# An FFT and mixer block on one core: the second channel product of most chunks from seven half-size products instead of eight

## The chip, the cores and the metric

The kernel runs on one core of one Trainium2 chip. The metric is the device time of one execution in microseconds; the time before is a median of three runs. The engines are named as in the profile: PE is TensorE's matmuls and PEld its weight loads, DVE is VectorE, ACT is ScalarE, POOL is GpSimd, SP is SyncE, which here only issues DMAs.

## The reference

```python
def _attn_ref(x):                       # x: (8, 3008, 256)
    X = np.fft.fft(x, axis=1)
    X = np.fft.fft(X, axis=2)
    return X.real.astype(np.float32)

def _moe_ref(x, w_tok1, w_tok2, w_ch1, w_ch2):
    xt = x.transpose(0, 2, 1)
    h = np.maximum(xt @ w_tok1, 0.0) @ w_tok2      # (3008,256), (256,3008)
    u = x + h.transpose(0, 2, 1)
    h2 = np.maximum(u @ w_ch1, 0.0) @ w_ch2        # (256,1536), (1536,256)
    return (u + h2).astype(np.float32)

reference = _moe_ref(_attn_ref(x), ...)
```

The change concerns the last product, `relu(u @ w_ch1) @ w_ch2`, and the sum with `u` behind it.

## The kernel before, in words

The eight batches run one behind the other. Each has a front part (the Fourier transforms as small matrix products `pz`, `pw`, `py`, the token mixing `pt` and `pu`), which ends in `ut`: u, transposed, with the 256 channels in two halves of 128 partitions and the tokens along the free axis. The channel part takes `ut` in 6 chunks of 512 tokens (448 in the sixth).

A chunk has 12 slots, one for each block `ct` of 128 of the 1536 hidden channels. In each slot `mm1` makes one block of the first channel product: two matmuls of 512 columns into the PSUM tile `pc` (three buffers), and a relu that moves it to the fp16 tile `c1`, on VectorE for every third block (line 565) and on ScalarE for the others (line 563). `c1` has two buffers: while the slots of a chunk make its `c1`, the second channel product `mm2` takes the `c1` of the chunk before (`prev`). At slots 2, 5, 8 and 11 it makes 128 tokens each: 12 matmuls with `c1` as weights and 256 columns of `wc2` moving (line 590), into half of a PSUM tile `po`. Behind each second of them VectorE adds `uT`, which is u with tokens on partitions, and writes `osb` (lines 598 and 599, drawn as L90, the helper's line); at slot 11 SP stores `osb` (line 612). `uT` comes from DMA transposes that SP issues at slot 4 of the chunk's own slots (line 574).

The instructions are issued in the order in which the Python loops write them, each engine runs its own in that order, and semaphores connect them. The front part of the next batch is a generator; between the slots `take` draws from it evenly, 45 pieces over the 71 slots of a batch (in batch 0 over the last 40), so that each slot carries 0.6 of a piece. The columns of a batch's transforms are added in pairs first (`fold`: adds of 96x512 fp16 within SBUF), for batches 0 and 1 on VectorE, for the later ones on GpSimd, all in one piece when 8 front pieces are through (slot 13), followed by the loads of x for the batch after (`load_x`). At the end of a batch's chunks GpSimd moves 64 leftover columns of `c1` between an even batch and the odd one behind it (`tail1`).

Of the kernel before, what the change touches and what calls it, by code (L numbers as in the profile page):

```python
# [36 lines left out]
def kernel(  # L37
# [34 lines left out]
    def dram(t, offset, ap):  # L72
        return bass.AP(tensor=t, offset=offset, ap=ap)
# [31 lines left out]
    def gdma(out_, in_):  # L105
        G.dma_start(out=out_, in_=in_)  # L106
# [193 lines left out]
    wc2 = const.tile([P, NCT, D], FP16, tag="wc2")  # L300

    HC = DCH // 2

# [7 lines left out]
    def load_rest():  # L311
        load_wc1(0)
        for th in range(2):
            gdma(w2n[:, th, :], dram(w2_t, th * P * S, [[S, P], [1, S]]))
        load_wc1(1)
        gdma(wc2[:], dram(wc2_t, 0, [[D, P], [P * D, NCT], [1, D]]))

    yrow = const.tile([3, 2, 8, 64], FP16, tag="yrow")
    state = {}
# [25 lines left out]
    NFOLD = 17  # L345

    def filler(n):
        pw = ps_out("filler")
        for _ in range(n):
            nc.tensor.matmul(pw[:, 0:P], lhsT=ident[:], rhs=lrot[:], start=True,  # L350
                             stop=True)
# [197 lines left out]
            for c in (2, 1, 0, 3, 4, 5):  # L549
                yield from tok2(c)  # L550

    def mm1(b, c, c1, ct, cts=None):
        ut = state[b]["ut"]
        n = min(CW, S - CW * c)
        cts = cts or (ct,)
        pcs = [ps_mm("pc") for _ in cts]
        for h in range(2):
            for pc, ct in zip(pcs, cts):
                nc.tensor.matmul(pc[:, 0:n], lhsT=wc1[:, h, ct * P:(ct + 1) * P],  # L559
                                 rhs=ut[:, c, h, 0:n], start=(h == 0), stop=(h == 1))  # L560
# [8 lines left out]
    def turn_u(b, c):  # L569
# [4 lines left out]
            nc.sync.dma_start_transpose(out=uT[:, 0:n // P, h, :], in_=ut[:, c, h, 0:n])  # L574
        return uT

    def mm2(b, c, c1, uT, ks, box):
        last = c == 5
        if last and b % 2 == 0 and ks == 3:
            return  # L580
        if ks == 0:
            box["osb"] = work.tile([P, 4, D], FP32, tag="osb", name="osb", bufs=3)
        osb = box["osb"]
        fine = last and b == BB - 1
        if ks % 2 == 0 or fine:
            box["po"] = ps_out("po")
        po = box["po"]
        o = 0 if fine else D * (ks % 2)
        for ct in range(NCT):
            nc.tensor.matmul(po[:, o:o + D], lhsT=c1[:, ct, ks * P:ks * P + P],  # L590
                             rhs=wc2[:, ct, :], start=(ct == 0), stop=(ct == NCT - 1))
        end = ks % 2 == 1 or last and b % 2 == 0 and ks == 2 or fine
        if end:
            k0, n = (ks, 1) if fine else (ks & ~1, 1 + ks % 2)
            src = po[:].rearrange("p (k d) -> p k d", k=2)[:, 0:n]
            uf = uT[:].rearrange("p k h d -> p k (h d)")[:, k0:k0 + n]
            dst = osb[:, k0:k0 + n]
            tt(dst[:, :, 0:129], src[:, :, 0:129], uf[:, :, 0:129], AT.add)
            tt(dst[:, :, 129:256], src[:, :, 129:256], uf[:, :, 255:128:-1], AT.add)
        if fine:  # L600
            for i in range(2 if ks < 3 else 1):
                (nc.sync if i == 0 else nc.scalar).dma_start(
                    out=dram(out_t, (b * S + 8 * c + i + 2 * ks) * D, [[NQ * D, 64], [1, D]]),
                    in_=osb[64 * i:64 * i + 64, ks, :])
            if ks == 3:
                nc.scalar.dma_start(
                    out=dram(out_t, ((b - 1) * S + NQ - 1) * D, [[NQ * D, 64], [1, D]]),
                    in_=osb[64:128, 3, :])
        elif ks == 3 or last and b % 2 == 0 and ks == 2:
            for i in range(2):  # L610
                nk = 4 if not last or b % 2 and i == 0 else 3
                nc.sync.dma_start(
                    out=dram(out_t, (b * S + 8 * c + i) * D,
                             [[NQ * D, 64], [2 * D, nk], [1, D]]),
                    in_=osb[64 * i:64 * i + 64, 0:nk, :])
            if last and b % 2:
                nc.sync.dma_start(
                    out=dram(out_t, ((b - 1) * S + NQ - 1) * D, [[NQ * D, 64], [1, D]]),
                    in_=osb[64:128, 3, :])

    def take(g, n):
        for _ in range(n):
            next(g, None)
# [26 lines left out]
    for k in range(6):  # L650
# [9 lines left out]
    w2v[1] = w2r[:]  # L660

    NFRONT = 45
    own_at = {1: 1, 2: 1, 4: 1, 12: 1, 15: 1, 18: 1, 20: 1, 22: 1, 24: 1, 27: 1, 30: 1, 33: 1,
              36: 1, 39: 1}
    prev = None
    for b in range(BB):
        nxt = front(b + 1) if b + 1 < BB else iter(())
        fold1 = fold(1, V) if b == 0 and BB > 1 else iter(())
        first, done, folded = (31 if b == 0 else 0), 0, False
        for c in range(NCH):  # L670
            c1 = work.tile([P, NCT, CW], FP16, tag="c1", name="c1", bufs=2)
            uT = None
            box = {}
            for ct in range(NCT):
                slot = NCT * c + ct
                if b == 0 and slot < 3:
                    if slot == 0:
                        mm1(b, c, c1, ct, range(3))
                else:
                    mm1(b, c, c1, ct)  # L680
                if ct == 4:
                    uT = turn_u(b, c)
                if prev is not None and ct % 3 == 2:
                    mm2(*prev, ct // 3, pbox)
                if b == 0:
                    take(own, own_at.get(slot, 0))
                    if 10 <= slot < 27:
                        take(fold1, 1)
                    if slot == 27 and BB > 2:
                        load_x(2)  # L690
                    if slot in (31, 33, 35, 37):
                        th, hb = (slot - 31) // 4, (slot - 31) // 2 % 2
# [16 lines left out]
            prev, pbox = (b, c, c1, uT), box  # L709
    for s in range(4):  # L710
        mm2(*prev, s, pbox)

# [29 lines left out]
```

## Time and profile before

| | |
|---|---|
| median of 3 runs | 627.99 us (627.88 to 628.25) |
| profiled execution | 628.33 us, span 626.6 us, clock 0.997 |
| PE busy | 608.9 us, 97% |
| PEld busy | 420.9 us, 67% |
| DVE busy | 344.8 us, 55% |
| ACT busy | 293.2 us, 47% |
| POOL busy | 170.4 us, 27% |

Rows of the profile give, for a group of instructions, the line, the engine, output<-inputs, the shape, the count, the busy time in us and the mean ns of one, then the idle time of the engine just before them and what ended it. A line can be a helper's: all adds of two tensors have L90, whatever engine they are on. Timeline rows begin with the start and the length in us. PE rows of matmuls overlap with one another, so the pitch of a matmul is read from the starts.

### The profile page before, as it was taken

How to read it: one execution, taken by the hardware profiler on the slowest of the kernel's cores; microseconds unless marked ns; L12 is line 12 of the kernel's file. 1: busy time of each engine (PE TensorE's matmuls, PEld its weight loads, DVE VectorE, ACT ScalarE, POOL GpSimd, SP SyncE). 2: the span in 40 equal slices, each digit the busy share in tenths (PEclk: the TensorE clock that was granted, in tenths of full speed). 3: DMA queues.
4: the chain of work that ended last, by engine and by line, in shares of the span. 5: the costliest groups of instructions: out<-in, count | busy, mean ns of one | idle time of the engine just before them, and what ended most of it. 6: DMA issues, size and time to landing. Idle time of an engine off the chain costs nothing.

```text
span 626.6 us, 11701 instructions
## 1 busy us (share of the span) xinstructions
PE 608.9 (97%) x4753; PEld 420.9 (67%) x4753; DVE 344.8 (55%) x728; ACT 293.2 (47%) x573; POOL 170.4 (27%) x231
## 2 busy tenths in 40 slices
PE   4899999999999999999999999999999999999997
PEld 3556676677667776667666776666766677666666
DVE  8668647634764356544665446653466535653343
ACT  8643553464435543454534544356443554344441
POOL 8401890292012900166010850039000000000000
PEclk9899999999999999999999999999999999999999
DMA  8993855338324482336432294252223334342434
GB/s 156 210 171 64 147 79 124 70 69 160 53 52 92 76 139 54 85 54 133 108 68 51 57 170 81 48 92 53 51 52 66 87 51 52 80 67 57 89 65 105
DMA packets 83366, 55.46 MB, mean 89 GB/s; under 512 B 53746, under 2 KB 80050, under 8 KB 82546
## 3 DMA queue, kind: packets, MB, share of 16 engines
q1 hardware_dynamic: 76816, 36.82, 30.8%
q0 software_dynamic: 6176, 17.63, 15.4%
q8 instruction: 37, 0.61, 0.4%
q10 hardware_dynamic: 320, 0.26, 0.2%
q14 instruction: 17, 0.14, 0.1%
HBM read 35.26 MB, written 24.64 MB: 96 GB/s over the span
## 4 chain that ended last, share of the span: by engine, by line
PE 95%; DMA 2%; DVE 1%; POOL 1%; ACT 0%; issue 0%; DVEq 0%
PE po L590 39%; PE pc L559 39%; PE pu L495 7%; PE pt L517 3%; PE pw L448 2%; DMA w1m<-in_moe_w_tok_dram 2%; PE py L474 2%; PE pz L424 1%; PE pw L450 1%; PE ph L405 0%; PE ph L403 0%; POOL xm L109 0%; DVE ix L86 0%; POOL w1p L106 0%; POOL w1m L106 0%
## 5 line engine op out<-in xcount | busy, mean ns | idle before, releaser
L559 PE MATMUL pc<-ut,wc 128*128 128x512 f16 (+1 forms) x1152 | 307.0, 375 | 0.8 <-ACT c L97 0.5
L97 ACT ACTIVATE c<-pc 128x512 f16<-128x512 f32 (+1 forms) x384 | 215.0, 587 | 195.2 <-PE pc L559 174.8
L590 PE MATMUL po<-wc,c 128*128 128x256 f16 x2256 | 276.3, 273 | 0.0
L590 PEld LDWEIGHTS <-c 128*128 128x128 f16 x2256 | 220.6, 98 | 63.3
L84 DVE TENSOR_SCALAR c<-pc 128x512 f16<-128x512 f32 (+1 forms) x192 | 130.1, 677 | 120.3 <-PE pc L559 119.7
L559 PEld LDWEIGHTS <-wc 128*128 128x128 f16 x1152 | 103.1, 98 | 69.2 <-issue 4.6
L90 DVE TENSOR_TENSOR osb<-po,uT 128x258 f32<-128x258 f32 (+1 forms) x196 | 71.7, 408 | 120.2 <-PE po L590 118.8
L90 DVE TENSOR_TENSOR ut<-pu,yt 128x512 f16<-128x512 f32 (+1 forms) x96 | 63.5, 672 | 11.0 <-PE pu L495 10.8
L90 POOL TENSOR_TENSOR eo<-fa,fb 96x512 f16<-96x512 f16 (+1 forms) x48 | 54.2, 1150 | 0.0
L97 ACT ACTIVATE w<-pw 128x257 f16<-128x257 f32 x90 | 34.5, 385 | 36.0 <-PE pw L450 35.9
L708 POOL COPY tail<-c 128x768 f16<-128x768 f16 x4 | 3.3, 823 | 172.0 <-ACT c L97 172.0
L495 PE MATMUL pu<-w2r,uu 128*128 128x512 f16 (+1 forms) x168 | 49.8, 379 | 0.0
L706 POOL COPY c<-tail 128x768 f16<-128x768 f16 x4 | 3.3, 824 | 140.1 <-PE po L590 140.1
L90 DVE TENSOR_TENSOR yt<-py,sqy 128x512 f16<-128x512 f32 x48 | 30.6, 681 | 2.3 <-ACT sqy L97 2.3
L97 ACT ACTIVATE z<-pz 128x480 f16<-128x480 f32 (+1 forms) x28 | 18.2, 686 | 26.7 <-PE pz L424 26.7
L495 PEld LDWEIGHTS <-uu 128*128 128x128 f16 x192 | 18.7, 98 | 16.1 <-DVE uv L90 0.6
L90 POOL TENSOR_TENSOR fa<-xp,xm 96x512 f16<-96x512 f16 x24 | 27.5, 1146 | 1.6 <-DMA xm<-in_x_dram,ix 1.6
L90 POOL TENSOR_TENSOR fb<-xm,xp 96x512 f16<-96x512 f16 x24 | 27.5, 1148 | 0.0
L448 PE MATMUL pw<-td,z 128*128 128x257 f16 x96 | 26.1, 279 | 1.2 <-DVE z L101 0.7
L97 ACT ACTIVATE sqy<-py 128x512 f32<-128x512 f32 x24 | 14.3, 597 | 26.7 <-PE py L474 15.8
L101 DVE CAST z<-pz 128x480 f16<-128x480 f32 (+1 forms) x36 | 23.5, 653 | 3.2 <-PE pz L438 2.1
L90 POOL TENSOR_TENSOR eo<-xp,xm 96x4 f16<-96x4 f16 x24 | 5.3, 219 | 70.6 <-PE pz L438 70.6
(136 smaller groups left out, 337.2 us busy)
## 6 DMA issues: line engine op xcount, KB each, us to landing
out_dram<-osb SPq DMA_DIRECT2D x83, 256.0 KB
xp<-in_x_dram POOLq DMA_DIRECT2D x14, 408.0 KB, 5.5
out_dram<-osb SPq DMA_DIRECT2D x11, 192.0 KB
uT<-ut SPq DMA_TRANSPOSE x96
w2n<-in_moe_w_tok_dram POOLq DMA_DIRECT2D x2, 752.0 KB, 12.6
w1p<-in_moe_w_tok_dram POOLq DMA_DIRECT2D x2, 384.0 KB, 8.4
wc<-in_moe_w_ch_dram POOLq DMA_DIRECT2D x1, 768.0 KB
xp<-in_x_dram POOLq DMA_DIRECT2D x2, 272.0 KB
```

What stands on the lines that cost most here:

```text
L84: eng.tensor_scalar(out=out_, in0=in_, scalar1=s1, scalar2=None, op0=op0)
L90: eng.tensor_tensor(out=out_, in0=a, in1=b, op=op)
L97: nc.scalar.activation(out=out_, in_=in_, func=func, scale=scale, **kw)
L101: V.tensor_copy(out=out_, in_=in_)
L424: nc.tensor.matmul(pz[:, 96 * k:96 * k + 96], lhsT=eo[:, t0 + k, c], rhs=t1r, start=True, stop=True)
L448: nc.tensor.matmul(pw[:, 0:257], lhsT=zg[:, 1, g], rhs=td1[:], start=True, stop=False)
L450: nc.tensor.matmul(pw[:, 0:129], lhsT=zg[:, 0, g], rhs=td0[:], start=False, stop=True)
L474: nc.tensor.matmul(py[:, P * k:P * k + P], lhsT=w[:, 4 * c + k, o:o + P], rhs=tab[:, 4 * c + k, :], start=True, stop=True)
L495: nc.tensor.matmul(pu[:, 0:64 * nk], lhsT=uu[:, th, h, :], rhs=w2[:, th, :, 8 * c:8 * c + nk], start=(th == 0), stop=(th == 1))
L517: nc.tensor.matmul(pt[:, o:o + n], lhsT=hw[:, g, c], rhs=w[:, g, w0:w0 + n], start=(g == 0), stop=(g == NG - 1))
L559: nc.tensor.matmul(pc[:, 0:n], lhsT=wc1[:, h, ct * P:(ct + 1) * P], rhs=ut[:, c, h, 0:n], start=(h == 0), stop=(h == 1))
L590: nc.tensor.matmul(po[:, o:o + D], lhsT=c1[:, ct, ks * P:ks * P + P], rhs=wc2[:, ct, :], start=(ct == 0), stop=(ct == NCT - 1))
```

## The change

Chunks 0 to 4 of batches 1 to 7, and chunks 2 to 4 of batch 0, get their second product by a scheme of seven products (Strassen's, in Winograd's form). The hidden channels are cut in two halves, the tokens in two halves (i = 0 and 1) and the output channels in two halves. `a11` and `a21` are the lower hidden channels of the two token halves, `a12` and `a22` the upper ones. Four joins on VectorE, each 128x1536 in fp16, make s1 = a21 + a22, s2 = s1 - a11, s3 = a11 - a21, s4 = a12 - s2. Five sums of the weights (`b22`, `t1w` to `t4w`) are made once, in batch 0, on GpSimd. Each of the seven products is 2 x 6 matmuls with 128 columns moving. They run at the slots 0, 2, 4, 6, 7, 9 and 11 of the next chunk and accumulate in two PSUM tiles, `pa` and `pb`; between them VectorE takes out the intermediate sums with u added (`q`) and the four quarters of `osb`. `osb` and `wc2` get one more column, since the upper output channels are written in reverse; `osb` has two buffers instead of three.

In a chunk whose `prev` goes this way all 12 relus run on ScalarE. The DMA transposes of `u` are issued at slot 10 of the chunk ahead. GpSimd's fold is cut into pieces of 4 or 5 generator steps (5, 5 and 7 in batch 0), each behind a one-column copy `hold` that reads s4 and so waits for the last join; the load of x follows the last piece.

```diff
-    def ps_out(name):
-        return psum.tile([P, 512], FP32, tag="o2", name=name, bufs=2)
+    def ps_out(name, k):
+        return psum.tile([P, 512], FP32, tag=f"o{k}", name=name, bufs=1)
...
+    def seven(b, c):
+        return c < NCH - 1 and (b > 0 or c >= 2)
+
+    def weight_sums():
+        G.tensor_copy(out=wc2[:, :, D:D + 1], in_=wc2[:, :, P:P + 1])
+        lo, hi = wc2[:, 0:NH], wc2[:, NH:NCT]
+        b12 = lo[:, :, D:P:-1]
+        G.tensor_copy(out=b22[:], in_=hi[:, :, D:P:-1])
+        tt(t1w[:], b12, lo[:, :, 0:P], AT.subtract, G)
+        tt(t2w[:], b22[:], t1w[:], AT.subtract, G)
+        tt(t3w[:], b22[:], b12, AT.subtract, G)
+        tt(t4w[:], hi[:, :, 0:P], t2w[:], AT.subtract, G)
...
-            if ct % 3:
+            if ct % 3 or joins:
                 act(c1[:, ct, 0:n], pc[:, 0:n], func=AFT.Relu)
...
+    def quads(c1):
+        v = c1[:].rearrange("p c (a i t) -> p c a i t", a=2, i=2)
+        return (v[:, 0:NH, :, 0], v[:, NH:NCT, :, 0], v[:, 0:NH, :, 1], v[:, NH:NCT, :, 1])
+
+    def sums(c1, box, k):
+        a11, a12, a21, a22 = quads(c1)
+        box[k] = work.tile([P, NH, 2, P], FP16, tag=f"s{k}", name=f"s{k}", bufs=1)
+        if k == 1:
+            tt(box[1][:], a21, a22, AT.add)
...
+    def product(dst, left, right, first):
+        for a in range(2):
+            for k in range(NH):
+                nc.tensor.matmul(dst[:, P * a:P * a + P], lhsT=left[:, k, a, :],
+                                 rhs=right[:, k, :], start=(first and k + a == 0),
+                                 stop=(k == NH - 1), skip_group_check=True)
...
+        if k == 0:
+            box["a"] = ps_out("pa", 0)
+            product(box["a"], a11, wc2[:, 0:NH, 0:P], True)
...
+        if k < 0:
+            tt(q[:, 0], pa, u[:, 0], AT.add)
+        elif k == 1:
+            pb = ps_out("pb", 1)
+            product(pb, a12, wc2[:, NH:NCT, 0:P], True)
+            tt(osb[:, 0, :, 0:P], halves(pb), q[:, 0], AT.add)
+        elif k == 2:
+            product(box["a"], box[2], t2w, False)
+            tt(q[:, 1], pa, u[:, 1], AT.add)
+        elif k == 3:
+            box["b"] = ps_out("pb", 1)
+            product(box["b"], box[1], t1w, True)
+        elif k == 4:
+            product(box["a"], box[3], t3w, False)
+            tt(q[:, 2], pa, u[:, 3], AT.add)
+            tt(osb[:, 1, :, D:P:-1], halves(box["b"]), q[:, 2], AT.add)
+        elif k == 5:
+            product(box["a"], a22, t4w, False)
+            tt(osb[:, 1, :, 0:P], pa, u[:, 2], AT.add)
+        elif k == 6:
+            product(box["b"], box[4], b22, False)
+            tt(osb[:, 0, :, D:P:-1], halves(box["b"]), q[:, 1], AT.add)
+            V.tensor_copy(out=box["osb"][:, :, P:P + 1], in_=box["osb"][:, :, D:D + 1])
+            store(b, c, box["osb"])
...
+    sum_at = {0: 1, 1: 2, 4: 3, 5: 4}
+    places = {0: 0, 1: -1, 2: 1, 4: 2, 6: 3, 7: 4, 9: 5, 11: 6}
...
+            fold_at = {42: 5, 54: 5, 66: 7} if b == 0 else {30: 4, 42: 4, 54: 4, 66: 5}
...
+            joins = prev is not None and seven(*prev[0:2])
...
-                if ct == 4:
+                if b == 0 and slot in (4, 16):
                     uT = turn_u(b, c)
-                if prev is not None and ct % 3 == 2:
+                if ct == (11 if b == 0 and c == 1 else 10) and (b, c) not in ((0, 0), (BB - 1, NCH - 1)):
+                    uT_next = turn_u(*divmod(NCH * b + c + 1, NCH))
+                if prev is not None and seven(*prev[0:2]):
+                    if ct in places:
+                        mm2_seven(*prev, places[ct], pbox)
+                    if ct in sum_at:
+                        sums(prev[2], pbox, sum_at[ct])
+                elif prev is not None and ct % 3 == 2:
                     mm2(*prev, ct // 3, pbox)
+                if slot == 1 and b == 0:
+                    weight_sums()
...
-                if done >= 8 and not folded:
-                    folded = True
+                if slot in fold_at:
                     if b + 2 < BB:
-                        take(fold(b + 2, G), NFOLD)
-                    if b + 3 < BB:
+                        if slot == min(fold_at):
+                            fold2 = fold(b + 2, G)
+                        G.tensor_copy(out=hold[:], in_=pbox[4][:, 0, 0, 0:1])
+                        take(fold2, fold_at[slot])
+                    if slot == max(fold_at) and b + 3 < BB:
                         load_x(b + 3)
```

The order of the instructions shows at three places what this does. First VectorE in chunk 2 of batch 1, before: four relus of that chunk (`c1_1777`), and the four adds for chunk 1, whose output is `osb_1834`.

```order
L84 TENSOR_SCALAR c1_1777<-pc_1778 128x512
L101 CAST z_1642<-pz_1782 128x4x24
L84 TENSOR_SCALAR c1_1777<-pc_1853 128x512
L90 TENSOR_TENSOR osb_1834<-po_1835,uT_1683 128x2x129
L90 TENSOR_TENSOR osb_1834<-po_1835,uT_1683 128x2x127
L84 TENSOR_SCALAR c1_1777<-pc_1890 128x512
L84 TENSOR_SCALAR c1_1777<-pc_1923 128x512
L90 TENSOR_TENSOR osb_1834<-po_1906,uT_1683 128x2x129
L90 TENSOR_TENSOR osb_1834<-po_1906,uT_1683 128x2x127
```

The same engine with the change, where chunk 1's joins s1 to s4 and its adds stand; `c1_1945` is chunk 1's, and `uv` belongs to the front part.

```order
L90 TENSOR_TENSOR s1_2158<-c1_1945 128x1536
L90 TENSOR_TENSOR q_2156<-pa_2143,uT_1934 128x256
L90 TENSOR_TENSOR s2_2165<-s1_2158,c1_1945 128x1536
L90 TENSOR_TENSOR osb_2157<-pb_2175,q_2156 128x2x128
L90 TENSOR_TENSOR q_2156<-pa_2143,uT_1934 128x256
L90 TENSOR_TENSOR s3_2214<-c1_1945 128x1536
L90 TENSOR_TENSOR s4_2224<-c1_1945,s2_2165 128x1536
L90 TENSOR_TENSOR q_2156<-pa_2143,uT_1934 128x256
L90 TENSOR_TENSOR osb_2157<-pb_2234,q_2156 128x2x128
L90 TENSOR_TENSOR osb_2157<-pa_2143,uT_1934 128x2x128
L90 TENSOR_TENSOR uv_2329<-pt1_2302,squ_2327 128x128 x2
L84 TENSOR_SCALAR uu_2301<-uv_2329 128x256
```

The relus are gone from VectorE, and the joins and three `q` adds have come in; each add that reads `pa` or `pb` stands between two products on TensorE.

Second, GpSimd around the end of batch 0, before: the end of the fold of batch 2, the loads of x for batch 3, two copies, and the fold of batch 3 from its start without a break.

```order
L342 COPY e_89<-eo 96x1
L106 DMA xp<-in_x_dram 48x4352 x2
L109 DMA xm<-in_x_dram,ix_69 96x2048 x2
L467 COPY ut<-ut 128x2x64
L708 COPY tail_216<-c_1472 128x768
L90 TENSOR_TENSOR fa<-xp,xm 96x512
L90 TENSOR_TENSOR fb<-xm,xp 96x512
```

With the change, from the end of the fold of batch 2 to the second piece of that of batch 3:

```order
L342 COPY e_89<-eo 96x1
L106 DMA xp<-in_x_dram 48x4352 x2
L109 DMA xm<-in_x_dram,ix_69 96x2048 x2
L805 COPY tail_221<-c_1570 128x768
L797 COPY hold<-s_2224 128x1
L90 TENSOR_TENSOR fa<-xp,xm 96x512
L90 TENSOR_TENSOR fb<-xm,xp 96x512
L90 TENSOR_TENSOR eo<-xp,xm 96x4
L90 TENSOR_TENSOR eo<-fa,fb 96x4x128
L90 TENSOR_TENSOR eo<-fa,fb 96x4x127
L797 COPY hold<-s_2480 128x1
```

The fold of batch 3 now waits at each piece for the s4 of a chunk. Third, SP at the same place, before: transposes, then the store of the chunk ahead, one chunk apart.

```order
L574 DMA_TRANSPOSE uT<-ut 128x4x128 x2
L612 DMA out_dram<-osb 64x4x256 x2
L574 DMA_TRANSPOSE uT<-ut 128x4x128 x2
L486 DMA yrow<-yt 1x2x512 x2
L612 DMA out_dram<-osb 64x4x256 x2
```

With the change:

```order
L598 DMA out_dram<-osb 64x4x256 x2
L486 DMA yrow<-yt 1x2x512 x2
L591 DMA_TRANSPOSE uT<-ut 128x4x128 x2
L598 DMA out_dram<-osb 64x4x256 x2
L486 DMA yrow<-yt 1x2x512
```

The pair of transposes that stands ahead of a store is now that of the next chunk, so it has moved past the front part's small DMAs and comes right before the store.

More of the change, by code (lines that the diff above doesn't have):

```diff
@@ L550, in front, with mm1 @@
                 yield from tok2(c)
-    def mm1(b, c, c1, ct, cts=None):
+    NH = NCT // 2
+    b22, t1w, t2w, t3w, t4w = (const.tile([P, NH, P], FP16, tag=n, name=n)
+                               for n in ("b22", "t1w", "t2w", "t3w", "t4w"))
+    def seven(b, c):
[9 more added lines that the diff above has]
+        tt(t4w[:], hi[:, :, 0:P], t2w[:], AT.subtract, G)
+    def mm1(b, c, c1, ct, joins, cts=None):
         ut = state[b]["ut"]
@@ L575, in turn_u, with store @@
         return uT
+    def store(b, c, osb):
+        last = c == 5
+        for i in range(2):
+            nk = 4 if not last or b % 2 and i == 0 else 3
+            nc.sync.dma_start(
+                out=dram(out_t, (b * S + 8 * c + i) * D,
+                         [[NQ * D, 64], [2 * D, nk], [1, D]]),
+                in_=osb[64 * i:64 * i + 64, 0:nk, 0:D])
+        if last and b % 2:
+            nc.sync.dma_start(
+                out=dram(out_t, ((b - 1) * S + NQ - 1) * D, [[NQ * D, 64], [1, D]]),
+                in_=osb[64:128, 3, 0:D])
@@ new lines, in quads @@
+    def quads(c1):
[7 more added lines that the diff above has]
+        elif k == 2:
+            tt(box[2][:], box[1][:], a11, AT.subtract)
+        elif k == 3:
+            tt(box[3][:], a11, a21, AT.subtract)
+        else:
+            tt(box[4][:], a12, box[2][:], AT.subtract)
@@ new lines, in product, with halves, mm2_seven @@
+    def product(dst, left, right, first):
[4 more added lines that the diff above has]
+                                 stop=(k == NH - 1), skip_group_check=True)
+    def halves(ps):
+        return ps[:, 0:2 * P].rearrange("p (a d) -> p a d", a=2)
+    def mm2_seven(b, c, c1, uT, k, box):
+        a11, a12, a21, a22 = quads(c1)
+        u = uT[:].rearrange("p (a i) h d -> p (i h) a d", a=2)
+        if k == 0:
+            box["a"] = ps_out("pa", 0)
+            product(box["a"], a11, wc2[:, 0:NH, 0:P], True)
+            box["q"] = work.tile([P, 3, 2, P], FP32, tag="q", name="q", bufs=1)
+            box["osb"] = work.tile([P, 4, D + 1], FP32, tag="osb", name="osb", bufs=2)
+        pa, q = halves(box["a"]), box["q"]
+        osb = box["osb"][:].rearrange("p (a i) d -> p i a d", a=2)
+        if k < 0:
[4 more added lines that the diff above has]
+            tt(osb[:, 0, :, 0:P], halves(pb), q[:, 0], AT.add)
+        elif k == 2:
+            product(box["a"], box[2], t2w, False)
+            tt(q[:, 1], pa, u[:, 1], AT.add)
+        elif k == 3:
+            box["b"] = ps_out("pb", 1)
[12 more added lines that the diff above has]
+            store(b, c, box["osb"])
@@ L581, in mm2 @@
         if ks == 0:
-            box["osb"] = work.tile([P, 4, D], FP32, tag="osb", name="osb", bufs=3)
+            box["osb"] = work.tile([P, 4, D + 1], FP32, tag="osb", name="osb", bufs=2)
         osb = box["osb"]
@@ L585, in mm2 @@
         if ks % 2 == 0 or fine:
-            box["po"] = ps_out("po")
+            box["po"] = ps_out("po", ks % 2 if fine else ks // 2)
         po = box["po"]
@@ L607, in mm2 @@
                     out=dram(out_t, ((b - 1) * S + NQ - 1) * D, [[NQ * D, 64], [1, D]]),
-                    in_=osb[64:128, 3, :])
+                    in_=osb[64:128, 3, 0:D])
         elif ks == 3 or last and b % 2 == 0 and ks == 2:
[L610 to L619, printed above, removed]
+            store(b, c, osb)
     def take(g, n):
```

26 lines of the change are left out of this document (13 added, 13 removed).

## The prediction

> **What bounds the kernel now.** I read the page first, then the chain of waits, then the timeline of one engine at a time. The page says which engine is full:
>
> ```profile
> span 626.6 us, 11701 instructions
> PE 608.9 (97%) x4753; PEld 420.9 (67%) x4753; DVE 344.8 (55%) x728; ACT 293.2 (47%) x573; POOL 170.4 (27%) x231
> PE   4899999999999999999999999999999999999997
> PE 95%; DMA 2%; DVE 1%; POOL 1%; ACT 0%; issue 0%; DVEq 0%
> PE po L590 39%; PE pc L559 39%; PE pu L495 7%; PE pt L517 3%; PE pw L448 2%; DMA w1m<-in_moe_w_tok_dram 2%; PE py L474 2%; PE pz L424 1%; PE pw L450 1%; PE ph L405 0%; PE ph L403 0%; POOL xm L109 0%; DVE ix L86 0%; POOL w1p L106 0%; POOL w1m L106 0%
> ```
>
> TensorE is busy in every slice but the first two and the last, 95% of the chain that ended last is TensorE, and `po` (line 590), the product that is changed, is 39% of it. So time taken from that line comes off the end, as long as nothing else becomes late. TensorE's timeline in batch 1 gives the price of a matmul of each width; a row's start minus the next row's is the true pitch, since busy times of pipelined matmuls overlap:
>
> ```profile
> 144.31 0.85 PE L517 MATMUL pt<-w,hp 128*128 128x129 f16 x12
> 144.99 0.84 PE L517 MATMUL pt<-w,hq 128*128 128x127 f16 x12
> 145.67 0.59 PE L559 MATMUL pc<-ut,wc 128*128 128x512 f16 x2
> 146.10 0.18 PE L457 MATMUL prot<-w,lrot 128*128 128x12 f16 x1
> 146.55 1.47 PE L590 MATMUL po<-wc,c 128*128 128x256 f16 x12
> 147.86 0.59 PE L559 MATMUL pc<-ut,wc 128*128 128x512 f16 x2
> 148.08 0.88 PEld L517 LDWEIGHTS <-hp 128*128 128x128 f16 x12
> ```
>
> Twelve matmuls of 256 columns take 147.86 - 146.55 = 1.31 us, 109.2 ns each. Twenty-four of about 128 columns, each with weights of its own, take 145.67 - 144.31 = 1.36 us, 56.7 ns each, with the step to the next line in it. Two of 512 take 0.43 us, one slot of the first channel product.
>
> **The change, part by part.** *The products.* A chunk of the second channel product was 4 x 12 matmuls of 256 columns, 48 x 109.2 ns = 5.24 us. It becomes 7 products x 2 halves x 6 = 84 matmuls of 128 columns, each with its own weights, 84 x 56.7 ns = 4.76 us: 0.48 us less. Chunks 0 to 4 of batches 1 to 7 and chunks 2 to 4 of batch 0 change, 38 in all: 38 x 0.48 = 18.2 us. A rounding of 0.01 us in the two differences moves this by 38 x 0.05 = 2 us. The pattern of line 517 is the nearest row there can be: runs of twelve, fresh weights at each matmul, accumulation in one place, rows of 257 elements beneath.
>
> The Trainium skill (TensorE: Matmul & The Clock Gate, "Back-to-back issue gap") speaks against the change: in a sustained stream of weight loads and matmuls it gives about 81 ns for 128 columns, not the 56 ns of its formula for one alone. By that a chunk would cost 84 x 81 = 6.80 us, 1.56 us more than now, and the kernel 59 us more. The 56.7 ns of the row above disagrees, over runs of 24; no run here shows 84 nearly in a row.
>
> *What must stay hidden.* VectorE gets four joins of 128x1536 fp16 per chunk, seven adds of 128x256 instead of four of 258 and 254, and a copy of four elements; ScalarE gets the relus of the 38 following chunks.
>
> ```profile
> L97 ACT ACTIVATE c<-pc 128x512 f16<-128x512 f32 x320 | 181.3, 596 | 127.7 <-PE pc L559 108.8 <-issue 14.6 <-DMA xp<-in_x_dram 2.8
> L84 DVE TENSOR_SCALAR c<-pc 128x512 f16<-128x512 f32 x160 | 110.3, 689 | 102.4 <-PE pc L559 101.7 <-DMA xp<-in_x_dram 0.6
> L90 DVE TENSOR_TENSOR ut<-pu,yt 128x512 f16<-128x512 f32 x80 | 54.2, 683 | 11.0 <-PE pu L495 10.8
> L90 DVE TENSOR_TENSOR osb<-po,uT 128x258 f32<-128x258 f32 x90 | 38.5, 427 | 112.7 <-PE po L590 111.3 <-issue 1.4
> L90 DVE TENSOR_TENSOR fa<-xp,xm 96x512 f16<-96x512 f16 x8 | 3.3, 417 | 0.8 <-DMA xm<-in_x_dram,ix 0.8
> L90 DVE TENSOR_TENSOR eo<-xp 96x128 f16<-96x128 f16 x2 | 0.4, 218 | 0.0
> L458 DVE CAST w<-prot 128x12 f16<-128x12 f32 x8 | 1.6, 203 | 0.0
> L90 POOL TENSOR_TENSOR eo<-fa,fb 96x512 f16<-96x512 f16 x24 | 27.7, 1155 | 0.0
> ```
>
> No join is in the trace. The nearest rows are VectorE's fp16 adds within SBUF: 417 ns for 512 elements and 218 for 128, so 0.518 ns per element and, for 1536, 218 + 1408 x 0.518 = 947 ns. The other end is the rate of the fp32 rows (683 ns for 512, 1.0 ns per element above 128), 1.7 us. I take 0.95, since type and place are those of the fp16 rows. An add of 256 is 0.42, the copy 0.2 (the row of 12 elements). So a chunk gives VectorE 4 x 0.95 + 7 x 0.42 + 0.2 = 6.9 us, and takes away four relus (2.7) and four adds (1.7): 38 x 2.5 = 95 us more, 440 us of 610, 72%. ScalarE gets 152 relus of at most 0.596, 90 us, and comes to 383 us, 63%. In sum both fit; the question is the order within a chunk.
>
> I lay one chunk out by hand, without front work, as in batch 7, where TensorE is quickest. Time 0 is the end of the previous chunk's last product; a product is 0.68, a slot of the first channel product 0.43, an engine's step to the next 0.06. VectorE: last add 0.48, copy 0.68, s1 1.63, q0 2.05, s2 3.00, and product 2 would start on TensorE at 5 x 0.43 + 2 x 0.68 = 3.51, so 0.5 us are to spare. Product 2 ends at 4.19; q1 4.67, s3 5.62, s4 6.57; TensorE reaches product 4, which needs s3, at 6.16 (0.5 to spare). It ends at 6.84; q2 is read by 7.32, and product 5, which overwrites what q2 reads, would start at 7.70 (0.4). The last starts at 9.24 and the chunk ends at 9.92. TensorE never waits. ScalarE needs 12 x 0.596 = 7.2 of 9.92, and its last relu ends about time 0, before s1 asks for it. In chunks 4 and 5, the densest, about 7.6 adds `ut` come in: VectorE 6.9 + 7.6 x 0.68 = 12.1 us, TensorE 9.92 + 7.6 x 0.43 = 13.2. Once, in the last chunk of batch 0 with twelve of them, VectorE needs up to 15.1 and TensorE (448 columns there) 14.4: up to 0.7 us lost, I take 0.3.
>
> *The fold on GpSimd* moves from one piece behind slot 13 to pieces of 4 or 5 behind s4. What it would do beside a join is shown by another VectorE instruction whose data lie in SBUF alone:
>
> ```profile
> L84 DVE TENSOR_SCALAR uu<-uv x16: 293/294/1066, 33.4 to 521.0; 128x256 f16<-128x256 f32 x16
> 86.87 1.07 DVE L84 TENSOR_SCALAR uu<-uv 128x256 f16<-128x256 f32 x1
> 86.64 2.30 POOL L90 TENSOR_TENSOR eo<-fa,fb 96x512 f16<-96x512 f16 x2
> ```
>
> It takes 0.29 us, but 1.07 when GpSimd's add began 0.23 us ahead of it: it ends just after that add. The Trainium skill (SBUF — State Buffer, "Who interferes with whom") says that two-input VectorE work within SBUF shuts out, and is shut out by, a GpSimd instruction that reads SBUF; no run so far shows it for a join. Four pieces take 4 x 1.15 + 0.2 = 4.8 us. Behind s4 at 6.57 they end at 11.4; with front work chunks last 11 to 13 us and s4 comes later too. In chunk 3 of a batch I get an end at 13.1 against the next s1 at 13.0. There are 17 such pieces with joins behind them; at 0 to 0.45 us of waiting each (one instruction of 1.15 less the 0.5 to spare, less some overlap) 0 to 8 us; I take 0.5.
>
> The copy `hold` makes GpSimd wait for s4; behind it in its queue stand the fold pieces, the tail copies and the loads of x. The loads for batch b+3 now go out behind slot 66 instead of about slot 33 (17 steps of some 1.15 us behind slot 13), and are wanted at slot 30 of the next batch, 36 slots or over 30 us later, against 5.5 us to land (below): nothing.
>
> *The weight sums*, four adds of 768 elements on GpSimd in batch 0, about 1.7 us each by the row of 512, and two copies, meet VectorE's fold of batch 1 if the weights land late. Between no meeting and one for every second add this is 0 to 3 us, once; I take 0.5. *The transposes* of `u` are issued at slot 10 of the chunk before instead of slot 4 of their own, and are needed at slot 1 of the next, so they gain 6 slots. On SP's queue each pair now stands right ahead of a store:
>
> ```profile
> 164.31 3.66 SPq L574 DMA_TRANSPOSE uT<-ut  x2
> out_dram<-osb SPq DMA_DIRECT2D x83, 256.0 KB
> xp<-in_x_dram POOLq DMA_DIRECT2D x14, 408.0 KB, 5.5
> ```
>
> The store waits behind at most these 3.7 us, and with two `osb` instead of three it has from slot 11 to slot 2 of the chunk after next, over 12 us; a 408 KB transfer lands in 5.5. I cost both at nothing; without that cover, a late store would hold the first add of a chunk and by it product 3.
>
> **The sum**: -18.2 + 0.3 + 0.5 + 0.5 = -16.9. The profiled execution took 628.33 us with a span of 626.6, and the median is 627.99, 0.05% below it; from the median 611.1, say 611.
>
> **Rivals.** (1) *VectorE late.* If fold pieces meet the next s1 (8 us above), or the joins take 1.25 us rather than 0.95, the half microsecond to spare is used up and most chunks lose 0.1 to 0.3: 38 x 0.2 = 8. The result is 615 to 621. For it: the slack is thin and VectorE has never been so full; against it: my schedule uses whole durations, while VectorE's neighbours overlap. (2) *Joins at the slow rate, slower than before.* At 1.7 us, s2 ends at 0.68 + 1.7 + 0.42 + 1.7 = 4.5 against 3.51, so product 2 waits 1.0; q1 and s3 end 2.2 after product 2 against TensorE's 1.97, 0.2 more; s4 pushes q2 and holds product 5 by 0.5: 1.7 us per chunk, 38 x 1.7 = 65, less 18: 675. It decides from about 1.5 us per join, where the waits reach 0.48. The patterns of a join have three dimensions instead of two; the fp16 rows with reversed steps are fast all the same. (3) *Weight loads set the pitch* in long streams: the change breaks even at 5.24 / 84 = 62.4 ns per matmul. The load rows (0.88 us for 12, 73 ns, at the start of a run) are the only ones that point there; at 73 ns the chunk costs 6.13, and the time is 628 + 38 x 0.89 = 662. The skill's 81 ns, by the same working, would give 687.
>
> **How the numbers follow.** The main case, 608 to 614, gets 0.70; rival 1 0.14; more gain than that (VectorE's overlap, and pitches at the good end of the rounding) 0.03; rival 2 0.05; rival 3 0.04; something between that cancels the gain 0.04, of which 0.03 lies within 0.2%. A measurement of this kernel tells about 0.2%, 1.3 us, from no change. So faster 0.87, same 0.03, slower 0.10. The range 607 to 621 holds the first two, 0.84.
>
> **What would show it.** Right: 3192 matmuls of 128x128 at line 626 with a pitch of 57 ns; a full batch of some 71 us; joins near 0.95 us; DVE near 440 us, ACT near 380; PE still 9 in the slices, and its waits for s1 to s4 or q under 0.1 us. Rival 1 shows as TensorE's weight loads waiting for VectorE at line 626, with joins of about 2 us beside the fold; rival 2 as joins of 1.7 us; rival 3 as a pitch above 60 ns without waits. Wrong most easily: VectorE's order within a chunk.

## The result, and the profile after

The changed kernel takes 610.08 us (median of 4 runs, 609.21 to 611.09) against 627.98: 0.9715 of the time before, 95% interval 0.9696 to 0.9734. Measured again beside the last experiments it took 610.39, ratio 0.9731 (0.9715 to 0.9746). Executions of one kernel at a mean granted clock of 0.996 to 0.997 take 1.3 to 1.4 us longer than those at 1.000, and the medians mix the two: like against like, the change took off 17.2 us there. The forecast was 611.

The page after, with the lines that answer to those of before:

```profile
span 607.4 us, 14835 instructions
PE 588.5 (97%) x6121; PEld 420.6 (69%) x6121; DVE 438.8 (72%) x880; ACT 375.2 (62%) x725; POOL 181.8 (30%) x260
PE   3899899999999999999999999999999999999997
PE 83%; DVE 0%; DVEq 0%; issue 0%
PE pc L576 36%; PE pa L626 16%; PE pb L626 12%; PE po L681 6%; PE pu L495 6%; PE pt L517 3%; PE py L474 1%; PE pw L448 1%; PE pz L424 1%; PE pw L450 1%; DVE s L90 0%; DVE ut L90 0%; PE pz L438 0%; DVE osb L90 0%; DVEq L834 0%; PE pz L433 0%
```

TensorE is still the full engine. The chain could be followed back only to 100.8 us, which is 83% of the span, so its shares cannot be set beside those of before; where it could be followed, it runs along TensorE throughout. VectorE and ScalarE have taken what the working gave them, 438.8 and 375.2 us busy against 440 and 383. TensorE's timeline in batch 4:

```profile
372.02 0.83 PE L626 MATMUL pb<-b,s 128*128 128x128 f16 x12
372.69 0.39 PE L474 MATMUL py<-tp,w 128*128 128x128 f16 x4
373.34 0.84 PE L626 MATMUL pa<-wc,c 128*128 128x128 f16 x12
374.02 0.39 PE L474 MATMUL py<-tq,w 128*128 128x128 f16 x4
376.64 0.83 PE L626 MATMUL pa<-t2w,s 128*128 128x128 f16 x12
377.31 0.59 PE L495 MATMUL pu<-w2r,uu 128*128 128x512 f16 x2
```

Start to start, a product takes 0.67 us (55.8 ns per matmul), and 0.68 (0.675 and 0.677) where it reads `wc2`. A chunk is 5 x 0.67 + 2 x 0.68 = 4.71 us instead of 5.24. VectorE at the same place, and the groups of the joins and of the osb copy:

```profile
373.35 0.42 DVE L665 COPY osb<-osb 128x4 f32<-128x4 f32 x1
373.68 0.94 DVE L90 TENSOR_TENSOR s<-c 128x1536 f16<-128x1536 f16 x1
374.55 0.41 DVE L90 TENSOR_TENSOR q<-pa,uT 128x256 f32<-128x256 f32 x1
374.89 0.94 DVE L90 TENSOR_TENSOR s<-s,c 128x1536 f16<-128x1536 f16 x1
L90 DVE TENSOR_TENSOR s<-c 128x1536 f16<-128x1536 f16 x76 | 73.0, 960 | 1.1 <-ACT c L97 0.9
L90 DVE TENSOR_TENSOR s<-s,c 128x1536 f16<-128x1536 f16 x38 | 36.0, 946 | 0.0
L665 DVE COPY osb<-osb 128x4 f32<-128x4 f32 x38 | 10.6, 280 | 1.3
```

s2 ends at 374.89 + 0.94 = 375.83 and product 2, which needs it, starts at 376.64: 0.8 us to spare in this chunk. Over the full batches that room goes from 0.15 to 1.1 us. The tightest place is product 5 of the third chunk in batches 1 to 6, which starts 0.06 us after q2 has read what it overwrites:

```profile
155.38 0.41 DVE L90 TENSOR_TENSOR q<-pa,uT 128x256 f32<-128x256 f32 x1
155.85 0.83 PE L626 MATMUL pa<-t4w,c 128*128 128x128 f16 x12
```

The saving is steady in the full batches. The same matmul two batches apart, before and after:

```profile
218.90 0.85 PE L517 MATMUL pt<-w,hp 128*128 128x129 f16 x12
366.76 0.85 PE L517 MATMUL pt<-w,hp 128*128 128x129 f16 x12
```

```profile
215.00 0.85 PE L517 MATMUL pt<-w,hp 128*128 128x129 f16 x12
357.64 0.85 PE L517 MATMUL pt<-w,hp 128*128 128x129 f16 x12
```

147.86 us become 142.64, 0.52 us less for each of the ten chunks between. In batch 0 two stalls of TensorE have become longer or are new. The first one before, then both with the change:

```profile
73.32 0.28 PE L448 MATMUL pw<-td,z 128*128 128x257 f16 x1 [0.68 <-DVE z L101]
```

```profile
72.83 0.28 PE L448 MATMUL pw<-td,z 128*128 128x257 f16 x1 [1.54 <-DVE z L101]
102.32 0.59 PE L495 MATMUL pu<-w2r,uu 128*128 128x512 f16 x2 [0.83 <-DVE ut L90]
```

The first waits for a small copy of the front part, which now stands behind s1, q0 and s2 on VectorE; it adds 0.9 us to the 0.68 of before. The second is in the chunk with twelve `ut`.

### The profile page after: what moved, and what is told of

It reads as the page before. It is cut to its first block, busy times and chain, and to the rows that moved or that the text cites. A ratio compares the mean times of both kernels' runs of the same rounds, so it can differ in the third digit from the quotient of the medians.

```text
span 607.4 us, 14835 instructions
## 1 busy us (share of the span) xinstructions
PE 588.5 (97%) x6121; PEld 420.6 (69%) x6121; DVE 438.8 (72%) x880; ACT 375.2 (62%) x725; POOL 181.8 (30%) x260
## 4 chain that ended last, share of the span: by engine, by line
PE 83%; DVE 0%; DVEq 0%; issue 0%
PE pc L576 36%; PE pa L626 16%; PE pb L626 12%; PE po L681 6%; PE pu L495 6%; PE pt L517 3%; PE py L474 1%; PE pw L448 1%; PE pz L424 1%; PE pw L450 1%; DVE s L90 0%; DVE ut L90 0%; PE pz L438 0%; DVE osb L90 0%; DVEq L834 0%; PE pz L433 0%
## 5 line engine op out<-in xcount | busy, mean ns | idle before, releaser
L97 ACT ACTIVATE c<-pc 128x512 f16<-128x512 f32 (+1 forms) x536 | 301.8, 587 | 159.1 <-PE pc L576 139.1
L626 PEld LDWEIGHTS <-s 128*128 128x128 f16 x1824 | 114.6, 98 | 34.2 <-DVE s L90 0.7
L626 PEld LDWEIGHTS <-c 128*128 128x128 f16 x1368 | 86.3, 97 | 25.7
L90 DVE TENSOR_TENSOR q<-pa,uT 128x256 f32<-128x256 f32 x114 | 49.2, 432 | 39.8 <-PE pa L626 39.0
L90 DVE TENSOR_TENSOR s<-c 128x1536 f16<-128x1536 f16 x76 | 73.0, 960 | 1.1 <-ACT c L97 0.9
L90 DVE TENSOR_TENSOR osb<-pb,q 128x256 f32<-128x256 f32 x114 | 48.4, 425 | 29.6 <-PE pb L626 28.2
L681 PE MATMUL po<-wc,c 128*128 128x256 f16 x432 | 53.4, 273 | 0.0
L681 PEld LDWEIGHTS <-c 128*128 128x128 f16 x432 | 42.1, 97 | 12.6
L90 DVE TENSOR_TENSOR s<-c,s 128x1536 f16<-128x1536 f16 x38 | 36.1, 950 | 0.0
L90 DVE TENSOR_TENSOR s<-s,c 128x1536 f16<-128x1536 f16 x38 | 36.0, 946 | 0.0
L97 ACT ACTIVATE z<-pz 128x480 f16<-128x480 f32 (+1 forms) x28 | 18.2, 678 | 26.4 <-PE pz L424 26.4
L626 PE MATMUL pb<-wc,c 128*128 128x128 f16 x456 | 31.9, 219 | 0.0
```

Source lines behind the costliest of these rows:

```text
L90: eng.tensor_tensor(out=out_, in0=a, in1=b, op=op)
L97: nc.scalar.activation(out=out_, in_=in_, func=func, scale=scale, **kw)
L626: nc.tensor.matmul(dst[:, P * a:P * a + P], lhsT=left[:, k, a, :], rhs=right[:, k, :], start=(first and k + a == 0), stop=(k == NH - 1), s ...
```

## The experiments

The kernel before ran beside all of them, at 626.6 to 627.9 us (medians). Where an experiment is set against the changed kernel, the time of that is the 610.4 us that it took beside the last four.

A wait in a PE row counts from the end of the matmul ahead of it. A row of 128 columns lasts 0.22 us at a pitch of 0.056, so a stalled TensorE loses about 0.16 us more than the row says. The losses of TensorE below are taken from start to start, which has this in it, less the same in the changed kernel.

**One product more.**

```diff
             product(box["a"], a11, wc2[:, 0:NH, 0:P], True)
+            product(box["a"], a11, wc2[:, 0:NH, 0:P], True)
```

> Product 0 is issued twice in each of the 38 chunks; the second overwrites the first, so nothing else changes. Theory (TensorE sets the end and a product costs 12 matmuls at the pitch of about 56.3 ns read in the trace after, 0.675 us): 38 x 0.675 = 25.7 us more than the changed kernel, 635 to 637, and seven such products against 5.24 us are the whole gain. Rival (VectorE sets the end in many chunks, TensorE has some slack): clearly less than 25 us more, below 630.

Measured: 634.36 us, ratio 1.0118 (1.0099 to 1.0137), 24 us over the changed kernel; by the spans of the two profiles, 633.2 and 608.5, 24.7. So an added product shows nearly in full at the end: TensorE sets it, not VectorE, and eight products of 128 columns would have been slower than the kernel before. Of the missing microsecond 0.7 is in the two stalls of batch 0, which the longer chunks shorten.

**Everything but the seven products.**

```diff
-        return c < NCH - 1 and (b > 0 or c >= 2)
+        return False
...
-                        G.tensor_copy(out=hold[:], in_=pbox[4][:, 0, 0, 0:1])
```

> No chunk goes the new way: all use the old second product and the old relus. The rest of the change stays: transposes at slot 10 of the chunk before, the fold in pieces (without the copy hold, since there is no s4), two osb buffers with a padded row, weight sums. Theory (these parts are worth nothing by themselves): as the kernel before, 626.5 to 629.5. Rival (the moved transposes or the spread fold bring part of the gain): 620 to 625.

Measured: 631.94 us, ratio 1.0080 (1.0061 to 1.0098): 5 us slower than before, as neither theory had it. TensorE is busy throughout, but its old runs of twelve matmuls have become longer, first before, then here:

```profile
153.57 1.47 PE L590 MATMUL po<-wc,c 128*128 128x256 f16 x12
154.88 0.38 PE L559 MATMUL pc<-ut,wc 128*128 128x512 f16 x1
```

```profile
150.93 1.50 PE L681 MATMUL po<-wc,c 128*128 128x256 f16 x12
152.26 0.59 PE L576 MATMUL pc<-ut,wc 128*128 128x512 f16 x2
153.78 1.50 PE L681 MATMUL po<-wc,c 128*128 128x256 f16 x12
155.12 0.59 PE L576 MATMUL pc<-ut,wc 128*128 128x512 f16 x2
```

1.31 us against 1.33 to 1.34; by the means over the full batches, 1.310 against 1.336. The kernel has 188 such runs, and 188 x 0.026 = 4.9 us is the whole loss, so the moved transposes, the fold in pieces and the two `osb` buffers cost nothing that shows. What these matmuls read differently is the row of `wc2`, 257 elements instead of 256. That led to the next two.

**Rows of 258, with the seven products and without.**

```diff
-    wc2 = const.tile([P, NCT, D + 1], FP16, tag="wc2")
+    wc2 = const.tile([P, NCT, D + 2], FP16, tag="wc2")
```

> As e2_eight_products, with the row of 258. Theory (all of the 4 to 5 us by which that kernel was slower than the one before come from 188 runs of twelve matmuls at 1.33 instead of 1.31 us): 626.5 to 628, as the kernel before, within 0.2%. Rival (the moved transposes, the fold in pieces or two osb buffers cost something too): 630 or more.

Measured without the seven products: 630.21 us, ratio 1.0047 (1.0034 to 1.0061). The runs of twelve take 1.325 us on the mean, so a row that is a multiple of four bytes brings back a little under half.

```profile
150.43 1.49 PE L681 MATMUL po<-wc,c 128*128 128x256 f16 x12
151.76 0.59 PE L576 MATMUL pc<-ut,wc 128*128 128x512 f16 x2
```

By the starts of whole batches, 0.31 us of each 74 remain against the kernel before, where the row of 257 had 0.57. Eight batches make 2.5 us, and like against like, as in the result, the two kernels differ by 2.5 us as well. The theory's range is missed and the median lies at the rival's mark, but nothing is left over for the parts that the rival named. That 257 costs more than 258 is shown, since the row is all that changes between these two kernels. That the rest of the way to 256 is the row's as well is argued only: the kernel before differs in its PSUM tiles and in `osb` too.

> Only the row of the weights wc2 grows from 257 to 258 fp16 elements, so that every row starts at a multiple of four bytes. In the trace after, twelve matmuls of 256 columns from the row of 257 take 1.33 us, in the trace before, with 256, 1.31; products that read t1w to t4w (rows of 128) take 0.67 and those that read wc2 0.68. Theory (a row at an odd element costs about 1 ns per 128 columns read): 38 x 2 x 0.01 + 36 x 0.02 = 1.5 us less than the changed kernel of the same call, and all products at 0.67 and 1.31. Rival (the difference has another cause, as the smaller banks or the accumulation): no change.

Measured with the seven products: 609.79 us, ratio 0.9726 (0.9709 to 0.9742), not distinguishable from the changed kernel's 0.9731. A pair of batches shortens by 0.16 us, and the products that read `wc2` go from 0.675 and 0.677 to 0.670 and 0.674 us. The theory of the row holds in kind, but a row of 258 is worth some 0.6 us over the kernel, not 1.5.

**Relus left on VectorE.**

```diff
-            if ct % 3 or joins:
+            if ct % 3:
```

> The relus of every third block stay on VectorE in the joined chunks too. That puts 4 x 0.69 = 2.7 us of work into VectorE's 7 us per chunk. Theory (VectorE has only about 0.5 us to spare at its tightest place, product 5, and 1 us on the average in a chunk's sum): 0.3 to 1.2 us of waiting per chunk, 38 times: 621 to 655. Rival (whatever has room in the sum, 72% + 15%, is hidden): 610 to 612.

Measured: 623.17 us, ratio 0.9940 (0.9921 to 0.9960), 13 us over the changed kernel, though VectorE is busy only 518.5 us, 83%. TensorE loses 12.6 us, two thirds of it where the layout had the least to spare, at product 5, which waits for q2. Most of the rest is at the front part's `pw`, which waits once, 1.5 us, in the changed kernel (a row of the waits: engine, line, what it waited for, total, times, longest):

```profile
PE pa L626 <- DVE q L90: 6.3, 13, 0.6
PE pw L448 <- DVE z L101: 3.4, 4, 2.1
```

**The fold as before.**

```diff
-                if slot in fold_at:
...
+                if done >= 8 and not folded:
+                    folded = True
                     if b + 2 < BB:
-                        G.tensor_copy(out=hold[:], in_=pbox[4][:, 0, 0, 0:1])
-                        take(fold2, fold_at[slot])
+                        take(fold(b + 2, G), NFOLD)
```

> The fold runs as before the change: in one piece from slot 13 on, without waiting for s4, and the loads of x behind it. Theory (a join within SBUF and a GpSimd add within SBUF shut each other out for up to 1.15 us): the joins of chunks 1 and 2 of batches 1 to 5 and of the end of batch 0 grow to 1.5 to 2 us, TensorE waits some 0.3 to 0.6 us in each of these 12 chunks: 613 to 618. Rival (they do not meet, as GpSimd's adds and VectorE's adds from PSUM do not): joins stay at 0.95 us and the time at 609 to 611.

Measured: 619.11 us, ratio 0.9888 (0.9866 to 0.9910), 9 us over the changed kernel, a little above the range. Where a join meets a GpSimd add, both grow (timeline, all engines):

```profile
137.78 2.98 POOL L90 TENSOR_TENSOR eo<-fa,fb 96x512 f16<-96x512 f16 x2
138.02 1.73 DVE L90 TENSOR_TENSOR s<-s,c 128x1536 f16<-128x1536 f16 x1
139.80 0.84 PE L626 MATMUL pa<-t2w,s 128*128 128x128 f16 x12 [0.49 <-DVE s L90]
```

The join takes 1.73 instead of 0.95 us, two adds of GpSimd 2.98 instead of 2.30, and product 2 waits. Of the 152 joins 39 are over 1 us here and 4 in the changed kernel. TensorE loses 8.9 us, nearly all of it behind a join, a q or a copy on VectorE. The loads of x go out earlier too in this run, but TensorE waits for no DMA. So the placing behind `hold` is worth these 9 us.

**One join twice, and all four.**

```diff
             tt(box[2][:], box[1][:], a11, AT.subtract)
+            tt(box[2][:], box[1][:], a11, AT.subtract)
```

> Only the join s2 is issued twice, 0.87 to 0.95 us more for VectorE per chunk and the same later for product 2. Theory (hand layout with 0.5 us to spare before product 2 where there is no front work, in the trace after about 0.8 in a chunk with some): 0 to 0.45 us of waiting per chunk, 38 x 0.2 = 8 us: 612 to 625. Rival (the slack is much larger than laid out): 609 to 611.

Measured: 625.07 us, ratio 0.9961 (0.9946 to 0.9976): 15 us over the changed kernel, just above the range. In batch 7, without front work, product 2 waits 0.27 us:

```profile
582.83 0.84 PE L627 MATMUL pa<-wc,c 128*128 128x128 f16 x12
584.34 1.94 DVE L90 TENSOR_TENSOR s<-s,c 128x1536 f16<-128x1536 f16 x2
586.34 0.84 PE L627 MATMUL pa<-t2w,s 128*128 128x128 f16 x12 [0.27 <-DVE s L90]
```

The pair of joins takes 1.94 us where one takes 0.95, so 0.99 more. Product 2 starts 3.51 us after product 0, and 3.08 in the changed kernel (569.53 to 572.61 us), 0.43 later. So 0.56 us were to spare there, where the layout had 0.51.

> All four joins are issued twice, which prices a join at about 1.8 us, the slow end that the prediction named. Theory (its rival 2, 1.7 us of waiting per chunk at 1.7 us per join): 610 + 38 x 1.7 to 2.0 = 675 to 690; slower than before the change. Rival (VectorE's total of 584 us still fits below 610): under 630.

Measured, with each of the four joins issued twice: 708.26 us, ratio 1.1290 (1.1263 to 1.1317), 98 us over the changed kernel, 2.6 per chunk instead of 1.7 to 2.0. The waits are where rival 2 put them:

```profile
264.76 0.84 PE L627 MATMUL pa<-t2w,s 128*128 128x128 f16 x12 [1.06 <-DVE s L90]
271.87 0.83 PE L627 MATMUL pa<-t4w,c 128*128 128x128 f16 x12 [0.82 <-DVE q L90]
```

The front part is not what the layout lacked: in batch 7, which has none, a chunk takes 12.55 us from one product 2 to the next (677.03 to 689.58), and 9.88 in the changed kernel, 2.67 more. What it lacked is time on the way between the engines. It lets VectorE read a product 0.74 us after the product's start and TensorE start at once behind VectorE. In the changed kernel's batch 7, q2 starts 0.87 us after product 4, and the waiting products here start 0.06 us behind VectorE:

```profile
575.25 0.83 PE L626 MATMUL pa<-t3w,s 128*128 128x128 f16 x12
576.12 0.42 DVE L90 TENSOR_TENSOR q<-pa,uT 128x256 f32<-128x256 f32 x1 [0.48 <-PE pa L626]
576.78 0.83 PE L626 MATMUL pa<-t4w,c 128*128 128x128 f16 x12
```

That is 0.2 us for each of the three waits of a chunk, and 0.6 of the 0.7 to 1.0 us that were missing.

**The transposes late.**

```diff
-                if b == 0 and slot in (4, 16):
-                    uT = turn_u(b, c)
-                if ct == (11 if b == 0 and c == 1 else 10) and (b, c) not in ((0, 0), (BB - 1, NCH - 1)):
-                    uT_next = turn_u(*divmod(NCH * b + c + 1, NCH))
+                if ct == 4:
+                    uT = uT_next = turn_u(b, c)
```

> The transposes of u are issued at slot 4 of their own chunk again, everything else as changed. Theory (they land long before slot 1 of the next chunk, 9 slots later, so their move is worth nothing): 609 to 611.5. Rival (issued so late, they or the stores behind them hold the first adds of a chunk): 613 or more.

Measured: 633.90 us, ratio 1.0102 (1.0078 to 1.0126): 23.5 us over the changed kernel, slower than before the change. The theory falls. Five waits of 0.9 to 9.0 us, one in each of batches 1 to 5, make 18.2 us, and each follows the loads of x at the end of the batch ahead; where no load runs there is none. Around the longest one:

```profile
412.15 3.13 POOL L106 DMA_DIRECT2D xp<-in_x_dram  x6 [0.17 <-POOL e L342]
415.58 0.97 POOL L109 DMA_INDIRECT xm<-in_x_dram,ix  x1 [0.30 <-issue]
421.22 9.82 SPq L591 DMA_TRANSPOSE uT<-ut  x2
432.52 0.42 DVE L90 TENSOR_TENSOR q<-pa,uT 128x256 f32<-128x256 f32 x1 [9.43 <-DMA uT<-ut]
433.87 1.46 PE L626 MATMUL pa<-t2w,s 128*128 128x128 f16 x12 [9.01 <-DVE s L90]
437.15 1.49 PE L626 MATMUL pb<-t1w,s 128*128 128x128 f16 x12
441.43 0.83 PE L626 MATMUL pa<-t4w,c 128*128 128x128 f16 x12
```

The pair of transposes takes 9.8 us of issue beside the loads, where pairs away from them take 2.5 to 4.3, q0 stands ahead of s2 in VectorE's queue and waits for it, and s2 and product 2 wait behind. In two of the five places the granted clock is 0.50 afterwards, for 3.2 and 6.0 us; with half of that and 0.16 for each wait the five make some 23.6 us. In the changed kernel the transposes run beside the loads too, at 6.2 to 7.2 us of issue in five places, but they are issued at slot 10 of the chunk ahead, 15 slots before slot 1 where the first add needs them, instead of 9.

**The small copies to ScalarE.**

```diff
-            copy(b > 0 or half, zo, pz[:, 0:96].rearrange("p (u k) -> p u k", u=4))
+            copy(b > 1 or b == 0 and half, zo, pz[:, 0:96].rearrange("p (u k) -> p u k", u=4))
```

> Only in batch 0, where the front part of batch 1 runs: its two copies z of 128x96 go to ScalarE instead of VectorE. In the trace after TensorE stands 1.5 us at 72.8 us, since such a copy waits on VectorE behind two joins. Theory (this is one of two stalls in batch 0 that take back 2 to 3 us of the gain): 1.0 to 1.6 us less than the changed kernel, about 608.7. Rival (the stall moves to the next wait): no change.

Measured: 609.77 us, ratio 0.9708 (0.9695 to 0.9721), which the time alone cannot tell from the changed kernel's 0.9715 and 0.9731. The stall falls from 1.54 to 0.89 us, on ScalarE now, so the gain is 0.65 us at most, half of what the theory had.

**The changed kernel again, and a version with more.**

> The changed kernel itself, as the measure for the other runs of this call: 608.5 to 611.

Measured: 610.39 us, as given above.

```diff
+        if c == NCH - 1:
+            return b % 2 == 1 and b < BB - 1
-        return c < NCH - 1 and (b > 0 or c >= 2)
+        return b > 0 or c >= 2
...
+            if c == 5 and b % 2:
+                G.tensor_copy(out=c1[:, :, 448:512], in_=tail1[:])
```

with rows of 258 in `wc2` and `w`, and the small copies on ScalarE.

> A version meant to be faster: rows of 258 in wc2 and in w, the two small copies of batch 0 on ScalarE, and the seven products also for chunk 5 of batches 1, 3 and 5, whose 64 borrowed columns GpSimd copies in at the chunk's start. Theory: 1.5 (rows) + 0.3 (w) + 0.6 (copies) + 3 x 0.55 (chunks) = 4 us less than the changed kernel of the same call. Rival (joins in chunk 0, where the z copies of the front part run on VectorE, bring waits as in batch 0): 2 us less.

Measured: 606.73 us, ratio 0.9676 (0.9658 to 0.9693) to the kernel before, 3.7 us less than the changed kernel beside it, near the theory's 4. The parts were not measured apart in this run, and the rows of `wc2` alone are worth less than the theory's 1.5 by the run above. That the sum comes out is in part luck.

## Why the prediction was right, and where its steps were off

*The products.* 38 x 0.48 = 18.2 us was forecast; 5.24 - 4.71 = 0.53 us gives 20.1. The pitch taken from line 517, 56.7 ns, very likely carried a surcharge that the prediction saw ("rows of 257 elements beneath") and did not price: five of seven products read rows of 128 and run at 55.8, the two that read rows of 257 at 56.2 and 56.4. The other side of it was missed altogether: the 36 runs of `po` that stay take 0.025 us more each with the padded `wc2`, 0.9 us together.

*Rival 3* is out. The eighty-four matmuls of a chunk, all with weights of their own, hold 55.8 to 56.4 ns in runs of twelve, below the 62.4 at which the change breaks even. They are not in a row: wider matmuls stand between the products, and the longest stretch without one is 36 (431.64 to 433.67 us, 56.4 ns each) and, with one product more, 48 (374.55 to 377.26 us, 56.5). The Trainium skill (TensorE: Matmul & The Clock Gate, "Back-to-back issue gap") gives 81 ns for a sustained stream; up to 48 this trace disagrees and stands by the figure that the page has for a single gap, about 56. No run shows a longer stream.

*The joins* were put at 0.947 us and took 0.946 to 0.960. *Rival 2*'s condition did not come about, but its price is nearer 100 us than 65, for the time between the engines that the layout left out.

*The fold.* 0.5 us of waiting had been taken, and *rival 1* put 8 on it. No matmul of line 626 waits for VectorE in the changed kernel. Only the weight loads do, 0.7 us in all and beside running matmuls (the last columns of the group are its idle time and how much of it `s` ended):

```profile
L626 PEld LDWEIGHTS <-s 128*128 128x128 f16 x1824 | 114.6, 98 | 34.2 <-DVE s L90 0.7
```

Four joins are over 1 us, 1.17 at most. One of them, 1.10 us at 83.4 us, has a GpSimd add beside it; the three of 1.16 to 1.17 have none and overlap with a `z` copy on VectorE itself. So the fold cost nothing in the end, and the rival came within the 0.15 and 0.06 us given with the profile after. That the wait behind s4 matters was shown by undoing it, 9 us. The Trainium skill (SBUF — State Buffer, "Who interferes with whom") has VectorE's two-input adds within SBUF and GpSimd's reads of SBUF shut each other out; the 1.73 us join beside the 2.98 us pair agrees.

*The thin slack* was real: in batch 7 0.56 us before product 2 for 0.51 laid out, and 0.24 before product 5 (576.54 to 576.78 us) for 0.38. In the full batches product 5 is where four relus more per chunk broke it.

*Batch 0.* 0.3 us for the dense chunk and 0.5 for the weight sums were taken. The weight sums cost nothing: they end at 43.8 us, and no matmul waits for them. The dense chunk cost 0.8, and the 0.9 us that the wait for the small copy grew by were not foreseen: the layout was made for a full batch, and the front part of batch 1 meets its first joins at another point.

*The transposes* were costed at nothing, which is what they cost in the change. But the working named the store as the work that needs cover. What needed it were the transposes themselves: the change also moves the loads of x beside them, and without the early issue that takes 23.5 us. The prediction looked at when the loads are wanted and not at what they pass on the DMA queues.

*The sum*, by these sizes: 20.1 - 0.9 - 0.9 - 0.8 = 17.5. That the forecast had 16.9 is in part luck: its products were 1.9 us short and the padded row was missing, 0.9 the other way, while its 1.3 us for chunk, weight sums and fold stand where 1.7 came from other places. The two profiles differ by 19.2 us. Of that 1.75 is the start, which varies between executions: the first `pt` starts at 31.05 us before, at 29.30 after and at 30.47 in the second profile of the changed kernel, and the granted clock from 20 to 24 us is 0.58, 1.00 and 0.72 in these three. That leaves some 17.4, which the sum meets.

## What to carry to other kernels

A saving in matmul columns is real on a full TensorE if the narrower matmuls keep their pitch: look for a row of that width, with fresh weights, in the same trace before believing or refusing it. What such a change moves elsewhere has to fit in order, not only in sum: here 83% on VectorE already cost 13 us, and the place was the one with the least to spare in a chunk laid out by hand. When a transfer is moved, price the transfers that it now runs beside, as well as those who wait for it.

## What the runs showed of the hardware

Twelve matmuls of 256 columns take 1.336 us, start to start, where the row of the moving operand has 257 fp16 elements, 1.325 where it has 258 and 1.310 where it has 256, means over the full batches: 2.2 and 1.3 ns more per matmul. From 257 to 258 nothing else changed; 256 stands in a kernel that differs elsewhere too. For 128 columns the same step from 257 to 258 took a run of twelve from 0.675 to 0.670 us on the first half of `wc2` and from 0.677 to 0.674 on the second.

After a long wait TensorE ran at half its clock. Behind the 9.01 us wait above a run of twelve took 1.46 to 1.49 us instead of 0.83, at a granted clock of 0.50, for 6.0 us. Behind one of 4.77 us in the same kernel it lasted 3.2 us:

```profile
132.90 1.46 PE L626 MATMUL pa<-t2w,s 128*128 128x128 f16 x12 [4.77 <-DVE s L90]
136.12 0.83 PE L626 MATMUL pb<-t1w,s 128*128 128x128 f16 x12
```

Behind one of 2.61 us the granted clock stayed at 1.00.
